# A list of single operations that runs to the 28th hidden step instead of the 16th, with six vector operations given to GpSimd

## The chip, the cores and the metric

The kernel runs on one core of one Trainium2 chip. The metric is the device time of one launch in microseconds (us), the median of several runs. A core has TensorE (PE in the profile: matrix products; PEld its weight loads), VectorE (DVE), ScalarE (ACT), GpSimd (POOL) and SyncE (SP), which here issues nearly all DMAs. Each engine works through its own instructions in the order in which they were written for it.

## What is computed

```python
def _attn_ref(x, state):                      # x: 8,8,512,64  state: 8,8,32,64
    scores = scale * x @ state^T              # softmax over the 32 states -> a
    xread = a @ state
    scores2 = scale * state @ x^T             # softmax over the 512 tokens -> a2
    sread = a2 @ x
    return concatenate([xread, sread], axis=2)
def _moe_ref(x, w_in, w_out):                 # 4352 tokens, 512 -> 2048 -> 512
    h = x @ w_in
    r = maximum(h, 0); return (r * r) @ w_out
def _moe2_ref(x, w_in, w_out, g_ln):          # 512 -> 1024 -> 512
    h = x @ w_in; solu = h * softmax(h)
    return (layernorm(solu) * g_ln) @ w_out
```

All inputs of the two feed-forward parts come in 64-bit floats; the output is 32-bit.

## The kernel before

The attention's read, `a @ state`, is never formed. For each batch the kernel multiplies `state` by the first weight matrix `w1in` (the products `sw`), and the hidden layer of a batch is then `a @ sw`. Every 32-bit operand of a matrix product is split into a high part and a low part (`high - rounded`), and a product takes three matmuls of 512 columns (lines 147 to 149 of `triple`).

**Steps.** The hidden layer of the first feed-forward part is made in steps: one step is one batch `b` and one block `f` of 128 of the 2048 hidden columns. A step has a hidden product (`hidden`, six matmuls into `ps_h`), a relu (`square`), a split of the square (`high` on ACT, `low` on DVE, tiles `gh` and `gl`), and four projections (`project`, three matmuls each into `acc`). Batches 0 and 1 take turns in chunks of four blocks, which makes the first 32 steps; batches 2 to 7 and the sread rows follow in 16 steps each.

**What the first 28 steps need besides.** 64-bit weights come by DMA as words and are turned into high and low parts (`convert_parts`, lines 215 to 232: six operations on DVE and two on ACT for each unit of 128 by 512 weights, 32 units in all, and for `w1in` a DMA that stores the result). `sw_part` multiplies state and weights, evicts on ACT (`ev_sw`, line 328) and stores to memory (`sw_d`, lines 334 to 340). `load_sw` reads a chunk back (`stg`, line 406), and `split_sw` or `split_part` splits it into `sw` (high part on ACT, low part on DVE: lines 122 and 123 when called in the list, 433 and 437 in a step). The attention of batches 0 and 1 is in `attention`, with row softmax in `rows_a` and `rows_b`; that of batch 2 is cut into parts that steps 18 to 32 hand out.

**What sets the order.** For PE, DVE, ACT and SP the order of instructions is that of the code. The first 16 steps are written as a list, `PLAN`: a piece is a letter and its indices (`H` hidden step, `G` and `L` high and low, `P` projection, `W` a state product, `V` a split of `sw`, `R`/`Q` row softmax, `i`/`o` weight conversion, `l` a load of a chunk). A piece issues one or more operations, on several engines, in one go. From step 16 the function `step` writes the order by fixed rules. GpSimd has its own order and only makes a few setup fills in the stretch spoken of here.

Of the kernel before, what the change touches and what calls it, by code (L numbers as in the profile page):

```python
# [20 lines left out]
def memory_attention_relu2_solu(  # L21
# [15 lines left out]
    nc = tc.nc  # L37
# [170 lines left out]
    def convert_parts(st, hi_r, lo_r, done=None):  # L208
# [30 lines left out]
    def convert_w1in(u, st):  # L239

        c, k = divmod(u, NM)

        t = u_tile("w1in")

        def done():
            nc.sync.dma_start(out=w1i_d[k][:, :, c * FC : (c + 1) * FC], in_=t.bitcast(F32))
            w1u[u] = t

        flying.append(convert_parts(st, t[:, 0, :], t[:, 1, :], done))

    w1o = []

    def convert_w1out(f, st):
        if f % 2 == 0:
            w1o.append(w_tile("w1out"))
        o = (f % 2) * 512
        flying.append(convert_parts(st, w1o[-1][:, 0, o : o + 512], w1o[-1][:, 1, o : o + 512]))
# [32 lines left out]
    def state_step(a, t):  # L290
# [9 lines left out]
        for i in range(2):  # L300
            if t == 0:
                split(bdw[0][:, i, :, i], bdw[0][:, i, :, 2 + i], v[:, :, :, :, i])
            else:
                o = bd[i][t]
                split(o[:, :, i], o[:, :, 1 - i], v[:, :, :, :, i])
# [4 lines left out]
    def sw_part(u, j):  # L310
# [6 lines left out]
        if at == 0:  # L317
            sw_ev[0] = evp.tile([P, 2, 512], F32, tag="ev", name="ev_sw")
        ev = sw_ev[0]
# [7 lines left out]
        triple(ps, [(lh, ll, t[:, 0, :], t[:, 1, :])], True, True)  # L327
        nc.scalar.activation(out=ev[:, at, :], in_=ps, func=AF.Copy)
        if single and j == 0:

            for b in range(2):
                if hp == 0:
                    loading[b, 0] = stgp.tile([P, 2, 512], F32, tag="stg", name="stg")
# [47 lines left out]
    def late_part(u, i):  # L381
        c, k = divmod(u, NM)
        if i == 0:
            sw_ev[0] = evp.tile([P, 2, 512], F32, tag="ev", name="ev_sw")
        ev = sw_ev[0]
# [33 lines left out]
    def split_sw(b, c):  # L419
        st = loading[b, c]  # L420
        loaded[b, c] = []
        for q in range(NQ):
            t = sw_tile("sw")
            split(t[:, 0, :], t[:, 1, :], st[:, q, :])
            loaded[b, c].append(t)
            if q == NQ - 1:
                loading.pop((b, c))
# [29 lines left out]
    def load_x(b):  # L457
        if b == 1:
            xs = wp.tile([P, NT, H, D], F32, tag="w", name="xs1")
        else:  # L460
            xs = xbuf.rearrange("p (t h d) -> p t h d", t=NT, h=H)
        for t in range(NT):
            nc.sync.dma_start(out=xs[:, t], in_=x[b].rearrange("h (p t) d -> t p h d", t=NT)[t])
        xs_t[b] = xs
# [25 lines left out]
    def attention(b):  # L490
# [5 lines left out]

        def trans_x(hp):
            if b >= 2:
                xt = atp.tile([P, S], F32, tag="st", name="xt", bufs=4)
                nc.vector.transpose(out=xt, in_=xq(hp))  # L500
                xh = xtp.tile([P, S], F32R, tag="xh", name="xh")
                xl = xtp.tile([P, S], F32R, tag="xl", name="xl")
                split(xh, xl, xt)
                v["xt", hp] = (xh, xl)
                return
            ps = ps_a.tile([P, 512], F32, tag=f"acc{hp}", name="ps_x")
            transposes(ps, [xs_t[b][:, t, 2 * hp : 2 * hp + 2].rearrange("p h d -> p (h d)") for t in range(NT)])
            if b == 0:
                xh = gp.tile([P, S], F32R, tag="gh", name="xh")
                xl = gp.tile([P, S], F32R, tag="gl", name="xl")  # L510
            else:

                if hp == 0:
                    new_a1()
                xh, xl = (a1_t[b][k][:, hp % 2, :] for k in range(2))
            v["rest", "x", hp] = split_bank(xh, xl, ps)
            v["xt", hp] = (xh, xl)

        def scores_t(hp):
            xh, xl = v.pop(("xt", hp))  # L520
# [3 lines left out]
            if b < 2:  # L524
                if i == 0:
                    v["ps", q] = bank("ps_s")
                lh, ll = (bdw[0][:, i, q, k : k + 2].rearrange("p l n b -> p (l n) b")[:, :, b] for k in (0, 2))
                triple(v["ps", q], [(lh, ll, xh, xl)], i == 0, i == 1)
                if i == 1:
                    nc.scalar.activation(out=v["st", q], in_=v["ps", q], func=AF.Copy)  # L530
                return
            ps = bank("ps_s")
            lt = bd[i][b // 2][:, q].rearrange("p l n b -> p (l n) b")[:, :, b % 2]
            nc.tensor.matmul(out=ps, lhsT=lt, rhs=xh, start=True, stop=False)
            nc.tensor.matmul(out=ps, lhsT=lt, rhs=xl, start=False, stop=True)
            n = 2 * NS
            r, o = i * n, (1 - i) * n
            st = v["st", q][r : r + n]
            nc.scalar.activation(out=st, in_=ps[o : o + n], func=AF.Copy)
            nc.vector.tensor_tensor(out=st, in0=ps[r : r + n], in1=st, op=ALU.add)  # L540
# [9 lines left out]
        def rows_a(tp):  # L550

            if b < 2:
                ps = bank("ps_r")
                by_token(tp, ps)
            else:
                ps = atp.tile([P, 512], F32, tag="e", name="e1")
                nc.vector.transpose(out=ps, in_=v["st", tp])
# [3 lines left out]
            e = atp.tile([P, 512], F32, tag="e", name="e1") if b < 2 else ps  # L561
# [3 lines left out]
            )  # L565
            nc.scalar.activation(out=e, in_=e, func=AF.Exp, scale=scale)
            v["e1", tp] = e

        def rows_b(tp):
            e3 = v["e1", tp].rearrange("p (g n) -> p g n", n=NS)  # L570
            sm = smp.tile([P, 2 * H], F32, tag="sm", name="sm")
            nc.vector.tensor_reduce(out=sm, in_=e3, axis=AX.X, op=ALU.add)
            nc.vector.tensor_scalar_add(sm, sm, 1e-9)
            nc.vector.reciprocal(out=sm, in_=sm)
            nc.vector.tensor_tensor(
# [3 lines left out]
        def cols_a(q):  # L579
# [3 lines left out]
            nc.vector.tensor_scalar_mul(mx, mx, -scale)  # L583
            sm = smp.tile([P, 1], F32, tag="cs", name="cs")
# [3 lines left out]
        def cols_b(q):  # L588
            st, sm = v["st", q], v["cs", q]
            nc.vector.tensor_scalar_add(sm, sm, 1e-9)  # L590
            nc.vector.reciprocal(out=sm, in_=sm)
            nc.scalar.activation(out=st, in_=st, func=AF.Copy, scale=sm)

        def cols_t(tp):
            ps = bank("ps_c")
            by_token(tp, ps)
            e = atp.tile([P, 2, H * NS], F32, tag="e", name="e2")
# [3 lines left out]
        def sread(half):  # L601
            if half == 0:
# [6 lines left out]
            for hp in (2 * half, 2 * half + 1):  # L609
                for t in range(NT):  # L610
                    for i in range(2):
# [7 lines left out]
                        )  # L619
            if half == 1:  # L620
                nc.scalar.activation(
# [923 lines left out]
```

## Time and profile before

| | |
|---|---|
| median of 3 runs | 1058.01 us (1054.23 to 1058.95) |
| profiled execution, its own time | 1060.5 us |
| its span, first to last instruction | 1058.7 us |
| TensorE busy | 1027.7 us, 97% of the span |
| VectorE, ScalarE, GpSimd busy | 783.9, 634.9, 138.9 us |
| hidden step 16 begins, step 28 begins | 126.5 us, 192.7 us |

The profiled execution takes 1.8 us more than its span, and 2.5 us more than the median of the runs. Matmuls are pipelined: a record of 0.39 us can begin 0.23 us after the one before, so that busy time is not the same as full use.

### The profile page before, as it was taken

How to read it: one execution, taken by the hardware profiler on the slowest of the kernel's cores; microseconds unless marked ns; L12 is line 12 of the kernel's file. 1: busy time of each engine (PE TensorE's matmuls, PEld its weight loads, DVE VectorE, ACT ScalarE, POOL GpSimd, SP SyncE). 2: the span in 40 equal slices, each digit the busy share in tenths (PEclk: the TensorE clock that was granted, in tenths of full speed). 3: DMA queues.
4: the chain of work that ended last, by engine and by line, in shares of the span. 5: the costliest groups of instructions: out<-in, count | busy, mean ns of one | idle time of the engine just before them, and what ended most of it. 6: DMA issues, size and time to landing. Idle time of an engine off the chain costs nothing.

```text
span 1058.7 us, 14931 instructions
## 1 busy us (share of the span) xinstructions
PE 1027.7 (97%) x5142; PEld 847.0 (80%) x5142; DVE 783.9 (74%) x1373; ACT 634.9 (60%) x1063; POOL 138.9 (13%) x168
## 2 busy tenths in 40 slices
PE   5899998999999999999999999999999999999998
PEld 4688776888888888888888888897888888888877
DVE  6899979777677578588686554578977877877871
ACT  6899776556556565465464443465765665666562
POOL 1000000000000000000000022222232233234110
PEclk9899999999999999999999999999999999999999
DMA  9769798387388395452531413633544444444441
GB/s 253 263 234 301 263 237 238 123 224 210 124 235 227 124 262 169 99 146 89 130 90 56 144 60 115 204 105 115 194 145 163 166 139 150 167 162 142 143 133 50
DMA packets 182956, 174.54 MB, mean 165 GB/s; under 512 B 98784, under 2 KB 132832, under 8 KB 182880
## 3 DMA queue, kind: packets, MB, share of 16 engines
q1 hardware_dynamic: 182160, 173.33, 52.9%
q8 instruction: 40, 0.66, 0.2%
q10 hardware_dynamic: 720, 0.26, 0.1%
q14 instruction: 36, 0.29, 0.1%
HBM read 106.43 MB, written 66.06 MB: 163 GB/s over the span
## 4 chain that ended last, share of the span: by engine, by line
PE 80%; DVE 9%; DMA 5%; ACT 2%; issue 2%; SPq 1%; POOL 1%; DVEq 0%; ACTq 0%; POOLq 0%
PE b L975 14%; PE acc L147 10%; PE acc L149 10%; PE acc L148 10%; PE ps_h L147 5%; PE ps_o L1118 5%; PE ps_o L1116 5%; PE ps_o L1117 5%; PE ps_h L149 5%; PE ps_h L148 5%; DMA sw_d<-ev_sw 1%; PE ps_sr L613 1%; DVE ch L225 1%; DMA st64w<-in_moe_w_in_dram 1%; DMA stg<-sw_d 1%
## 5 line engine op out<-in xcount | busy, mean ns | idle before, releaser
L147 PE MATMUL acc<-gh,w1out 128*128 128x512 f32 (+1 forms) x576 | 219.6, 381 | 2.9 <-DVE ev_x L854 1.6
L149 PE MATMUL acc<-gh,w1out 128*128 128x512 f32 (+1 forms) x576 | 217.9, 378 | 0.0
L148 PE MATMUL acc<-gl,w1out 128*128 128x512 f32 (+1 forms) x576 | 217.8, 378 | 0.0
L811 ACT ACTIVATE r<-ps_h 128x512 f32<-128x512 f32 (+1 forms) x144 | 82.1, 570 | 123.3 <-PE ps_h L149 122.5
L830 DVE TENSOR_TENSOR gl<-r,gh 128x512 fp32r<-128x512 f32 (+1 forms) x144 | 96.7, 672 | 60.1 <-ACT gh L825 53.7
L147 PEld LDWEIGHTS acc<-gh,w1out 128*128 128x128 f32 x576 | 108.7, 189 | 24.4 <-DVE ev_x L854 2.8
L149 PEld LDWEIGHTS acc<-gh,w1out 128*128 128x128 f32 x576 | 108.6, 189 | 20.5
L815 DVE TENSOR_TENSOR r<-r,ps_h 128x512 f32<-128x512 f32 (+1 forms) x120 | 77.6, 647 | 63.7 <-ACT r L811 62.8
L148 PEld LDWEIGHTS acc<-gl,w1out 128*128 128x128 f32 x576 | 108.7, 189 | 19.9
L825 ACT ACTIVATE gh<-r 128x512 fp32r<-128x512 f32 (+1 forms) x120 | 72.1, 601 | 71.2 <-DVE r L815 71.2
L1118 PE MATMUL ps_o<-w,ll 128*128 128x512 f32 x272 | 106.3, 391 | 1.3 <-DVE ll L1097 1.0
L1116 PE MATMUL ps_o<-w,lh 128*128 128x512 f32 x272 | 106.2, 390 | 0.1
L1117 PE MATMUL ps_o<-w,lh 128*128 128x512 f32 x272 | 105.9, 389 | 0.0
L149 PE MATMUL ps_h<-ah,sw 128*128 128x512 f32 x256 | 100.9, 394 | 3.4 <-DVE sw L437 2.2
L147 PE MATMUL ps_h<-ah,sw 128*128 128x512 f32 x256 | 103.0, 402 | 0.0
L148 PE MATMUL ps_h<-al,sw 128*128 128x512 f32 x256 | 100.5, 393 | 0.0
L203 POOL TENSOR_TENSOR cw<-cw,ce 128x512 f32<-128x512 f32 x16 | 20.7, 1294 | 543.9 <-DVE ce L200 500.9
L975 PE MATMUL b<-w,x2h 128*128 128x512 f32 x272 | 84.1, 390 | 0.3 <-DVE hB L993 0.3
L1048 POOL TENSOR_TENSOR var<-var,mhalf 128x1 f32<-128x1 f32 x34 | 43.6, 1281 | 234.7 <-DVE var L1047 234.5
L1118 PEld LDWEIGHTS ps_o<-w,ll 128*128 128x128 f32 x272 | 51.0, 188 | 13.4 <-DVE ll L1097 2.7
L149 PEld LDWEIGHTS ps_h<-ah,sw 128*128 128x128 f32 x256 | 48.5, 189 | 14.7 <-DVE sw L437 2.6
L1027 ACT ACTIVATE e<-hA,nm 128x1024 f32<-128x1024 f32 x17 | 19.6, 1151 | 67.2 <-DVE nm L1022 67.2
(232 smaller groups left out, 2082.9 us busy)
## 6 DMA issues: line engine op xcount, KB each, us to landing
ln_d<-ln_sq SPq DMA_DIRECT2D x32, 512.0 KB, 3.2
ln_t<-ln_d SPq DMA_DIRECT2D x128, 128.0 KB, 2.8
stg<-sw_d SPq DMA_DIRECT2D x120, 128.0 KB, 3.1
sw_d<-ev_sw SPq DMA_DIRECT2D x28, 512.0 KB, 3.5
st<-in_moe_w_out_dram SPq DMA_DIRECT2D x24, 512.0 KB, 5.2
st_x<-x_d SPq DMA_DIRECT2D x34, 256.0 KB, 3.7
w1i_d<-w1in SPq DMA_DIRECT2D x16, 512.0 KB, 4.6
st<-in_moe_w_in_dram SPq DMA_DIRECT2D x16, 512.0 KB, 5.2
```

The source lines that it names most:

```text
L147: nc.tensor.matmul(out=ps, lhsT=lh, rhs=rh, start=first and i == 0, stop=False)
L148: nc.tensor.matmul(out=ps, lhsT=lh, rhs=rl, start=False, stop=False)
L149: nc.tensor.matmul(out=ps, lhsT=ll, rhs=rh, start=False, stop=last and i == n - 1)
L811: nc.scalar.activation(out=r, in_=ps, func=AF.Relu)
L815: nc.vector.tensor_tensor(out=r, in0=r, in1=ps, op=ALU.mult)
L825: nc.scalar.activation(out=gh, in_=r, func=AF.Copy)
L830: nc.vector.tensor_tensor(out=gl, in0=r, in1=gh.bitcast(F32), op=ALU.subtract)
L975: nc.tensor.matmul(out=ps, lhsT=l, rhs=r, start=first and k == 0 and j == 0, stop=k == 1 and j == 2, skip_group_check=True,)
L1048: nc.gpsimd.tensor_tensor(out=var, in0=var, in1=mhalf, op=ALU.pow)
L1116: nc.tensor.matmul(out=ps, lhsT=a, rhs=wt[:, 0, o : o + 512], start=(k == 0), stop=False)
L1117: nc.tensor.matmul(out=ps, lhsT=a, rhs=wt[:, 1, o : o + 512], start=False, stop=False)
L1118: nc.tensor.matmul(out=ps, lhsT=bb, rhs=wt[:, 0, o : o + 512], start=False, stop=(k == NK - 1))
```

## The change

The list now goes on to the 28th step, and a piece no longer stands for a whole group of operations: each function yields after every operation or two, so that a name in the list issues the next operation of its piece, and the pieces of several engines can be interleaved one by one. The rules in `step` that served steps 16 to 27 are gone; the parts of batch 2's attention (`a...`), its loads (`q`, `h`), the partial sums read back (`x`) and the load of `gcol` (`g`) are names in the list too. Two kinds of operation change their engine: the low parts of the first state chunk (`split_sw` with `c == 0`, four operations) and the scaling of batch 0's row softmax (`rows_b` with `b == 0`, two operations) go from VectorE to GpSimd. The number of instructions on PE, ACT and SP stays the same; VectorE has six fewer and GpSimd six more.

```diff
@@ convert_parts (likewise state_step, trans_x, scores, rows_a, trans_a, hidden_part, project)
         nc.vector.tensor_scalar(out=zu, in0=hi, scalar1=0x7FFFFE00, scalar2=None, op0=ALU.bitwise_and)
+        yield 1
         nc.scalar.activation(out=zi, in_=zi, func=AF.Relu, scale=8.0, bias=rebias)
-
+        yield 1
...
@@ split_sw
-            split(t[:, 0, :], t[:, 1, :], st[:, q, :])
+            nc.scalar.activation(out=t[:, 0, :], in_=st[:, q, :], func=AF.Copy)
             loaded[b, c].append(t)
+            yield 1
+            (nc.gpsimd if c == 0 else nc.vector).tensor_tensor(
+                out=t[:, 1, :], in0=st[:, q, :], in1=t[:, 0, :].bitcast(F32), op=ALU.subtract
+            )
...
@@ rows_b
-            nc.vector.tensor_tensor(
+            yield 1
+            (nc.gpsimd if b == 0 else nc.vector).tensor_tensor(
                 out=e3, in0=e3, in1=sm.unsqueeze(2).to_broadcast([P, 2 * H, NS]), op=ALU.mult
             )
...
@@ before the list
-    nc.sync.dma_start(out=gcol, in_=g_ln.rearrange("(k p) -> p k", p=P))
...
-    when = {("o", f): w for f, w in zip(range(12, NF), (20, 21, 22, 23))}
-    when |= {("i", u): w for u, w in zip(range(3 * AHEAD + 1, NU), (16, 17, 18))}
...
@@ the list
-    I0 X0 J0 I2 i0 J2 X1 i0 U0 O0 O1 T02 T00 i0 i1 N02 T03 i2 N00 Z W00 S02 T01 N03 i2 N01 i1 i1 S00 i3 S03
...
+    I0 X0 i0 i0 i0 I2 i0 i0 i0 X0 i2 X0 i2 U0 U0 X0 i2 i2 T00 J0 i2 U0 U0 i2 i2 T01 i0 T00 T02 J2 T01 i0 i2
...
+    def piece(p):
+        if p not in steps:
+            steps[p] = parts(p[0], [int(c, 16) for c in p[1:]])
+        next(steps[p], None)
...
-    steady = range(4 * FPC, (B - 1) * NF)
+    steady = range(7 * FPC, (B - 1) * NF)
```

Three places show what this moves.

**GpSimd, from the setup fills on.** `cw`, `ce` belong to the later weight conversion. Before:

```order
masks.py:199 AFFINE_SELECT ident<-ident 128x128
L891 MEMSET a_st 128x1536
L892 MEMSET mhalf 128x1
L203 TENSOR_TENSOR cw<-cw,ce 128x512 x16
L920 TENSOR_TENSOR st_b<-st_b 128x1024 x3
```

and now:

```order
masks.py:199 AFFINE_SELECT ident<-ident 128x128
L903 MEMSET a_st 128x1536
L904 MEMSET mhalf 128x1
L587 TENSOR_TENSOR e_416<-e_416,sm 128x512
L587 TENSOR_TENSOR e_430<-e_430,sm 128x512
L435 TENSOR_TENSOR sw<-stg,sw 128x512 x4
L207 TENSOR_TENSOR cw<-cw,ce 128x512 x16
```

Six operations stand between the fills and the later conversion: the two softmax tiles of batch 0 (`e`), and then four low parts of `sw`.

**TensorE, just ahead of the first hidden product** (`ps_h`; `ps_a` are the softmax rows turned, `ps_s` scores, `ps_r` scores by token of batch 1, `ps_sw` state products). Before:

```order
L138 MATMUL ps_a_512<-ident,e_414 128x128 x2
L138 MATMUL ps_a_512<-ident,e_444 128x128 x2
L130 MATMUL ps_a_498<-ah,negi 128x512
L130 MATMUL ps_a_512<-ah,negi 128x512
L147 MATMUL ps_sw<-w1in,bd_1_189 128x512
L148 MATMUL ps_sw<-w1in,bd_1_189 128x512
L149 MATMUL ps_sw<-w1in,bd_1_189 128x512
L130 MATMUL ps_x<-ah,negi 128x512
L147 MATMUL ps_h<-ah,sw 128x512
```

and now:

```order
L147 MATMUL ps_s<-ah,bdw 128x512
L148 MATMUL ps_s<-al,bdw 128x512
L149 MATMUL ps_s<-ah,bdw 128x512
L147 MATMUL ps_s<-ah,bdw 128x512
L148 MATMUL ps_s<-al,bdw 128x512
L149 MATMUL ps_s<-ah,bdw 128x512
L516 MATMUL ps_a_532<-ah,negi 128x512
L147 MATMUL ps_sw<-w1in,bd_1_189 128x512
L148 MATMUL ps_sw<-w1in,bd_1_189 128x512
L149 MATMUL ps_sw<-w1in,bd_1_189 128x512
L558 MATMUL ps_r<-ident,st 128x128 x8
L147 MATMUL ps_h<-ah,sw 128x512
```

Batch 1's scores, its turn by token and the later state products now stand ahead of the first hidden product instead of behind it: 15 more matmuls of 512 columns (58 against 43) and eight more transposes (64 against 56).

**SyncE's queue at the fourth hidden chunk, of batches 1 and 0** (`sw_d` stores or loads of one head pair each, `stg` the chunk read back, `x2p_d` partial sums, `xs` the inputs of batch 2 or 3). Before:

```order
L406 DMA stg<-sw_d_57 64x512
L406 DMA stg<-sw_d_58 64x512
L406 DMA stg<-sw_d_59 64x512
L406 DMA stg<-sw_d_60 64x512
L170 DMA st_1865<-in_moe_w_out_dram 128x1024
L861 DMA x2p_d_117<-ev_x_1901 128x1024
L861 DMA x2p_d_117<-ev_x_1916 128x1024
L470 DMA xs<-in_x_dram 128x4x64 x4
L406 DMA stg<-sw_d_57 64x512
L406 DMA stg<-sw_d_58 64x512
L406 DMA stg<-sw_d_59 64x512
L406 DMA stg<-sw_d_60 64x512
```

and now:

```order
L353 DMA sw_d_60<-ev_sw 256x1x512
L414 DMA stg<-sw_d_57 64x512
L414 DMA stg<-sw_d_58 64x512
L414 DMA stg<-sw_d_59 64x512
L414 DMA stg<-sw_d_60 64x512
L414 DMA stg<-sw_d_57 64x512
L414 DMA stg<-sw_d_58 64x512
L414 DMA stg<-sw_d_59 64x512
L414 DMA stg<-sw_d_60 64x512
L170 DMA st_2003<-in_moe_w_out_dram 128x1024
L483 DMA xs<-in_x_dram 128x4x64 x8
L253 DMA w1i_d_65<-w1in 256x1x512
```

The second chunk's four loads stood behind a weight load, two partial sums and four input loads; they now follow the first chunk's directly. On DVE, the low part that step 24 needs was the engine's 296th instruction and is now its 285th; that of step 16 was the 228th and is the 209th, that of step 28 the 325th and the 310th.

## Rows read from the trace of the kernel before

**Rows 1.** The page: TensorE's busy time, and its granted clock in 40 slices.

```profile
PE 1027.7 (97%) x5142; PEld 847.0 (80%) x5142; DVE 783.9 (74%) x1373; ACT 634.9 (60%) x1063; POOL 138.9 (13%) x168
PEclk9899999999999999999999999999999999999999
```

**Rows 2.** Stretches: us, busy us (instructions) of each engine, granted clock, DMA share, GB/s.

```profile
0.00:8.20 8.20, 0.04 (x1) 0.07 (x2) 2.54 (x5) 2.52 (x4) 4.06 (x12) 1.00 0.82 176
8.20:30.00 21.80, 16.57 (x80) 12.03 (x80) 18.26 (x35) 17.49 (x34) 0.00 (x0) 1.00 0.99 305
30.00:40.70 10.70, 7.96 (x23) 5.57 (x24) 9.69 (x22) 7.87 (x17) 0.00 (x0) 0.58 0.68 236
40.70:120.00 79.30, 79.23 (x472) 65.00 (x472) 75.00 (x152) 70.19 (x131) 0.00 (x0) 0.99 0.76 259
120.00:180.00 60.00, 53.32 (x218) 40.99 (x217) 51.26 (x94) 41.12 (x74) 0.00 (x0) 0.97 0.87 254
```

**Rows 3.** Who PE waited for to 40.7 us: us in total, times, longest.

```profile
PE ps_st L296 <- DMA a_st<-in_state_dram: 8.2, 1, 8.2
PE ps_x L130 <- ACT ah L127: 1.8, 2, 1.0
```

**Rows 4.** PE from 123 us in order of time: start, us; in brackets idle, releaser.

```profile
128.34 0.50 PE L149 MATMUL ps_h<-ah,sw 128*128 128x512 f32 x1 [1.22 <-DVE sw L123]
155.13 0.51 PE L667 MATMUL ps_s<-xh,bd 128*128 128x512 f32 x1 [1.07 <-ACT ev_sw L328]
165.19 0.50 PE L147 MATMUL acc<-gh,w1out 128*128 128x512 f32 x1 [1.39 <-DVE ev_x L854]
174.79 0.61 PE L149 MATMUL ps_h<-ah,sw 128*128 128x512 f32 x1 [2.16 <-DVE sw L437]
```

**Rows 5.** The chain that ended last from 120 to 182 us: start, us, what.

```profile
128.92 6.60 DMA stg<-sw_d
149.58 4.82 DMA sw_d<-ev_sw
156.11 8.21 DMA sw_d<-ev_sw
170.18 3.14 DMA xs<-in_x_dram
174.04 0.70 DVE sw L437
175.83 0.43 PE ps_h L148
179.16 0.23 PE acc L148
```

**Rows 6.** The page, DMA issues: number, KB each, median us from issue to landing.

```profile
stg<-sw_d SPq DMA_DIRECT2D x120, 128.0 KB, 3.1
sw_d<-ev_sw SPq DMA_DIRECT2D x28, 512.0 KB, 3.5
```

**Rows 7.** Ahead of the first hidden step: PE and ACT in order of time.

```profile
33.17 0.69 PE L138 MATMUL ps_a<-ident,e 128*128 128x128 f32 x2 [1.26 <-DVE e L575]
39.20 0.63 PE L147 MATMUL ps_h<-ah,sw 128*128 128x512 f32 x1
38.29 0.59 ACT L131 ACTIVATE al<-ps_a 128x512 fp32r<-128x512 f32 x1
```

**Rows 8.** GpSimd's tensor operations and VectorE beside them, by time; then a group.

```profile
249.30 1.30 POOL L203 TENSOR_TENSOR cw<-cw,ce 128x512 f32<-128x512 f32 x1 [22.91 <-DVE ce L200]
249.86 1.29 DVE L697 TENSOR_TENSOR e<-e,mx 128x512 f32<-128x512 f32 x1
321.65 1.29 POOL L203 TENSOR_TENSOR cw<-cw,ce 128x512 f32<-128x512 f32 x1 [24.85 <-DVE ce L200]
322.05 0.67 DVE L740 TENSOR_REDUCE cm<-st 128x1 f32<-128x512 f32 x1
L575 DVE TENSOR_TENSOR e<-e,sm 128x512 f32<-128x512 f32 x4 | 2.8, 692 | 0.1
```

More of the change, by code (lines that the diff above doesn't have):

```diff
@@ L173, in memory_attention_relu2_solu, with run @@
     flying = []
+    def run(g):
+        for _ in g:
+            pass
     def advance():
@@ L495, in new_a1, with a1 @@
             a1_t[b] = tuple(a1p.tile([P, NQ, S], F32R, tag=t, name=t) for t in ("ah", "al"))
-        def trans_x(hp):
[L498 to L505, printed above, removed]
+        def a1():
+            if b not in a1_t:
+                new_a1()
+            return a1_t[b]
@@ L510, in trans_x, with low_x @@
+        def low_x(hp):
+            ps, xh = v["px", hp], v["xh", hp]
+            nc.tensor.matmul(out=ps, lhsT=negi, rhs=xh, start=False, stop=True, skip_group_check=True)
+            yield 1
+            if b == 0:
                 xl = gp.tile([P, S], F32R, tag="gl", name="xl")
             else:
[L513 to L517, printed above, removed]
@@ L519, in scores_t, with scores @@
-        def scores_t(hp):
-            xh, xl = v.pop(("xt", hp))
+                xl = a1()[1][:, hp % 2, :]
+            v["xl", hp] = xl
+            nc.scalar.activation(out=xl, in_=ps, func=AF.Copy)
+        def scores(hp):
+            xh, xl = v["xh", hp], v["xl", hp]
             q, i = hp // 2, hp % 2
             if i == 0:
-                v["st", q] = atp.tile([P, S], F32, tag="st", name="st", bufs=4)
[L524 to L540, printed above, removed]
@@ L601, in sread @@
         def sread(half):
-            if half == 0:
+            if "ps_sr" not in v:
                 v["ps_sr"] = bank("ps_sr")
@@ L1211, in memory_attention_relu2_solu, with hidden_part, high_part, parts @@
     done = []
-    att = [attention(0), attention(1)]
+    att, att2 = [attention(0), attention(1)], attention(2)
     steps = {}
-    hid, sq, ready, left = {}, {}, {}, {}
-    def piece(p):
-        k, a = p[0], [int(c, 16) for c in p[1:]]
+    hid, hid_ps, sq, ready, left = {}, {}, {}, {}, {}
+    def hidden_part(b, f):
+        ps = hid_ps[b, f] = hidden(b, f, loaded[b, f // FPC], *a1_t[b], S)
+        yield 1
+        r, rest = square(ps, S, f >= 3 * FPC)
+        hid[b, f] = b, f, S, r, f >= 3 * FPC
+        if f >= 3 * FPC:
+            yield 1
+            rest()
+    def high_part(b, f):
+        sq[b, f] = high(*hid[b, f])
+        r, times = hid.pop((b, f))[3:]
+        if not times:
+            yield 1
+            nc.scalar.activation(out=r, in_=r, func=AF.Square)
+    def parts(k, a):
         if k in "TNSRQABCDEF":
-            att[a[0]][k](a[1])
+            yield from att[a[0]][k](a[1])
         elif k in "io":
-            key = k, a[0]
-            if key not in steps:
-                begin(*key)
-                steps[key] = flying.pop()
-            next(steps[key], None)
+            yield from (convert_w1in if k == "i" else convert_w1out)(a[0], raw.pop((k, a[0])))
         elif k == "U":
-            state_step(a_st, a[0])
+            yield from state_step(a_st, a[0])
         elif k == "W":
-            sw_part(*a)
+            yield from sw_part(*a)
         elif k == "V":
-            key = tuple(a)
-            if key not in steps:
-                steps[key] = split_sw(*key)
-            next(steps[key], None)
+            yield from split_sw(*a)
         elif k == "H":
-            b, f = a
-            hid[b, f] = b, f, S, square(hidden(b, f, loaded[b, f // FPC], *a1_t[b], S), S, False)[0], False
-            done.append((b, f))
+            yield from hidden_part(*a)
         elif k == "G":
-            sq[a[0], a[1]] = high(*hid.pop((a[0], a[1])))
+            yield from high_part(*a)
         elif k == "L":
@@ L1502, in memory_attention_relu2_solu @@
     for m in range(4):
-        project(*pend[1], m)
+        run(project(*pend[1], m))
     sb.close()
```

246 lines of the change are left out of this document (141 added, 105 removed).

## The prediction

> **What bounds the kernel now.** I read the page first: TensorE is busy for 97% of the span, and its clock is below full in the second of 40 slices alone [rows 1]. So a change of order can only win where PE stands still or runs at the lower clock, and the next view, busy time by stretches, says where that is. PE is idle for 8.2 us to the first matmul, 5.2 of the next 21.8 us, 2.7 of the 10.7 us after that, 0.07 of 79.3 us in the middle, and 6.7 of 60 us from 120 to 180 us [rows 2]. From there to step 28 at 192.7 us, where the new list ends, it does not wait at all. In the waits of the first stretch the 8.2 us are for the state's DMA; the rest are short waits for ACT and DVE, 1.8 us in the largest group [rows 3].
>
> The four long waits after 120 us end with DVE or ACT: 1.2, 1.1, 1.4 and 2.2 us, 5.8 of the 6.7 us [rows 4]. The chain of waits shows what was late behind them. Chunk loads and stores that usually land 3.1 and 3.5 us after issue [rows 6] took 6.6, 4.8 and 8.2 us here, and the last wait ends behind a run of DVE work whose end is the low part of `sw` at 174.04 us [rows 5]. The stretch is thus limited by DVE's order and by DMAs that were asked for in a bunch, not by DVE's total: DVE is busy 51 of its 60 us [rows 2].
>
> The lower clock costs as well. At 1.2 GHz a matmul of 512 columns begins 0.43 us after the one before, at 2.4 GHz 0.23 us [rows 5]: 0.20 us for each. In the first such stretch (granted clock 0.58 from 30 to 40.7 us [rows 2]) some twelve of the 23 records are such matmuls, 2.4 us; after the 2.2 us wait at 174.79 us about eight, 1.6 us. To be had at most, then: 5.2 + 2.7 + 2.4 = 10.3 us before 40.7 us, nothing in the middle, and 6.7 + 1.6 = 8.3 us from 120 us on. The 8.2 us for the first DMA stay.
>
> **Part by part: the beginning.** No work is removed; PE, ACT and SP issue what they did. The new order puts 15 matmuls of 512 columns and eight transposes ahead of the first hidden product: 15 x 0.23 = 3.4 us, and eight of a quarter of the width, 0.5 us, together 3.9 us that PE now does in time that it waited through. Against that stands when the first hidden product can begin, 39.20 us before [rows 7]. It needs the softmax's scaled rows, which PE turns at 33.17 us right after DVE's scaling, then a split whose last piece ACT ended just before 39 us [rows 7]. In the new order ACT reaches that piece three operations later, three of 0.59 us [rows 7] or 1.8 us, but ACT was idle for 2.8 of the 10.7 us [rows 2]. The scaling runs on GpSimd: 1.29 us, as its operation on tiles of this size, against 0.69 us on DVE [rows 8], so 0.6 us more on this path. I take 0.8 us later in all (from 1.5 us earlier, if the loads that the list moves forward release it, to 3.5 us later, if nothing is absorbed: 1.8 + 0.6 and another 0.6 for the low part of `sw` with half a us of handing over). The beginning thus gives 3.9 - 0.8 = 3.1 us (0.4 to 5.4). I leave the low clock there, since PE still has many short gaps before its first hidden step; if it does not fall, 2.4 us more.
>
> **The six operations on GpSimd.** They free DVE of 6 x 0.69 = 4.1 us on paper. The trace shows what stands against this: a DVE operation with two inputs in SBUF that began beside GpSimd's took 1.29 us instead of the 0.69 us of the same form, and ended after it, while a reduction with one input beside GpSimd kept its 0.67 us [rows 8]. At 0.6 us for each of six that is 3.6 us back, so DVE gains about 0.5 us; I count nothing. The bounds are a gain of 4.1 us of DVE time, where only reductions or operations on PSUM lie beside them, and a loss of 6 x 1.29 - 4.1 = 3.6 us, where DVE stands still for all of each. The Trainium skill has this as a rule (SBUF — State Buffer, section "SBUF: two separate sides"): one pair of SBUF ports is shared by VectorE and GpSimd as an exclusive lock, which whoever comes first holds for the whole instruction. The trace agrees for two SBUF inputs; for VectorE's one-input operations in the fast mode, which the page counts in too, no row here shows it. By the page DVE would lose the 3.6 us, by the rows nothing.
>
> **From 120 us on.** Here the gain comes from order alone. Step 24 waits for a low part that was DVE's 296th instruction and is now the 285th; six of the eleven went to GpSimd, five were moved behind. At 0.69 us for a long operation and less for a short one that is some 6 us of DVE work, against a wait of 2.2 us [rows 4]. Step 16's is nineteen earlier, with a wait of 1.2 us [rows 4]. The four loads of the second chunk no longer stand behind two partial sums, which wait for an eviction, and the input loads are spread over the list, so that the bunch of DMAs behind the 8.2 us landing [rows 5] is thinner. The two waits for evictions, 1.1 and 1.4 us [rows 4], hang on that landing and are the less certain part. I take 6.5 of the 8.3 us: all but one wait of about the size of those that stand (2.5 us if only step 24's wait goes, 8.3 us if all go). What becomes late next is ACT: step 24's chunk is still loaded only some 9 us of matmuls ahead of its use, and its high parts go through ACT.
>
> **What the new order can spoil.** The middle has no idle time now. A list that names every operation binds each engine's order more tightly, and an engine that comes late by half a us holds all behind it. The old list cost 0.07 us of idle time in 79.3 us [rows 2]; I put 0.6 us against the new one (0 to 4 us, the size of the waits that stand after 120 us less the longest). `gcol`, now loaded late, is needed only at the second weights' conversion, after step 32.
>
> **Sum.** 3.1 + 0 + 6.5 - 0.6 = 9.0 us. The profiled execution of 1060.5 us would take 1051.5; its median stands 2.5 us lower, 1058.0, so the forecast is **1049.0 us**, a span of 1049.7. Its own range is 1045.5 to 1052.5.
>
> **Rivals.**
> - *More: the clock too.* The first stretch is dense enough that the clock does not fall, and nearly all waits go: 5.4 + 2.4 + 7.2 = 15 us, 1043 us. For it: the clock fell when PE had long waited in short pieces. Against: the transposes and splits of the start still alternate between PE and ACT.
> - *The beginning gives nothing.* The first hidden product comes 3.9 us later, held by ACT and GpSimd, and the rest holds: 6.5 - 0.6 = 5.9 us, less 0.4 us by which the clock stays low longer, 1052.5 us. For it: ACT has seven more operations to the first relu.
> - *Waits change places.* The chunk loads still come after stores that land late; the gaps after 120 us move to other steps, and the beginning gives 2 us: 1056 us, no change that counts. For it: DMA is 87% busy from 120 to 180 us [rows 2], and a bunch has to go somewhere.
> - *Slower: GpSimd's lock.* Up to the first hidden product five operations follow each other on GpSimd. If each first waits out a DVE operation, 5 x (1.29 + 0.69) = 9.9 us against 3.5 us on DVE puts it off by 6.4 us, 2.5 more than the 3.9 us of work moved forward; and if DVE stands still for all six, it is 3.6 us behind at 120 us, where PE already waits for it: 1058 + 6.1 = 1064 us. It decides if the first hidden product starts after about 45 us. For it: the pair at 249 us, DVE's end 0.5 us after GpSimd's [rows 8]. Against: much of DVE's work there reads PSUM or one input. [...]
>
> **Chances.** The forecast 0.48, more 0.13, nothing at the beginning 0.17, waits that change places 0.15, slower 0.07. A measurement of this kernel tells about 0.5%, 5.3 us, from no change: faster than 1052.7 us is the forecast nearly whole (0.45), the first rival and half of the second, 0.67; within it 0.26; slower 0.07. The range that holds it 8 times in 10 takes in the first rival's edge and most of the fourth's side, 1043.5 to 1056.5 us.
>
> **What would show it.** In the changed kernel's profile the first hidden product should begin near 40 us with 58 matmuls of 512 columns before it; GpSimd's six operations should take 1.3 to 2 us and some DVE operations beside them 1.2 us or more; PE's idle time from 120 us to step 28 should be under 2 us, without a low clock there, and step 28 should begin at about 183.7 us. From step 28 on the two traces should run alike. I am wrong if the first hidden product comes after 43 us, if the waits for `sw` and evictions are still there after 120 us, or if PE waits for more than 3 us between 41 and 120 us.

## The result and the profile after

The changed kernel takes 1045.43 us (median of 4 runs, 1044.1 to 1045.91) against 1057.16 us before (4 runs): a ratio of 0.989, with a 95% interval from 0.9864 to 0.9915. That is 11.7 us less. Its profiled execution takes 1045.91 us, with a span of 1044.1 us.

The page, in answer to [rows 1] (busy time; granted clock in 40 slices; the chain by engine) and [rows 6] (DMA issues):

```profile
PE 1021.6 (98%) x5142; PEld 844.4 (81%) x5142; DVE 779.0 (75%) x1367; ACT 632.6 (61%) x1063; POOL 146.3 (14%) x174
PEclk9999999999999999999999999999999999999999
...
PE 88%; DVE 5%; DMA 3%; ACT 2%; issue 1%; POOL 1%; ACTq 0%; SPq 0%; DVEq 0%; POOLq 0%
...
stg<-sw_d SPq DMA_DIRECT2D x120, 128.0 KB, 3.3
sw_d<-ev_sw SPq DMA_DIRECT2D x28, 512.0 KB, 3.4
```

The slice of lower clock is gone, and these two kinds of DMA take about as long to land as before (3.3 and 3.4 us against 3.1 and 3.5). The stretches of [rows 2] (us, busy us and instructions of PE, PEld, DVE, ACT and POOL, granted clock, DMA share, GB/s):

```profile
0.00:8.20 8.20, 0.00 (x0) 0.00 (x0) 3.05 (x7) 2.89 (x5) 4.06 (x12) 1.00 0.82 221
8.20:30.00 21.80, 18.89 (x88) 14.16 (x88) 19.36 (x42) 17.67 (x36) 1.74 (x2) 1.00 1.05 298
30.00:40.70 10.70, 9.50 (x46) 6.71 (x45) 10.47 (x16) 10.25 (x22) 4.81 (x4) 1.00 0.94 299
40.70:120.00 79.30, 76.89 (x460) 62.84 (x459) 72.11 (x148) 68.15 (x130) 1.33 (x1) 1.00 0.78 249
120.00:180.00 60.00, 60.00 (x266) 49.15 (x266) 56.56 (x111) 45.44 (x84) 0.00 (x0) 1.00 0.86 260
```

From 120 us on PE stands still for nothing: the waits of [rows 4] have no successors, and the chain there, in answer to [rows 5], is matmul after matmul. In the same 60 us PE begins 266 matmuls in place of 218, and DVE is busy 56.6 us in place of 51.3. From 30 to 40.7 us 46 records begin in place of 23, at full clock. The middle has lost, 2.4 us idle in place of 0.07. The waits that are left to 40.7 us ([rows 3]), and in the middle:

```profile
PE ps_st L303 <- DMA a_st<-in_state_dram: 9.0, 1, 9.0
PE ps_s L148 <- ACT al L540: 1.3, 1, 1.3
...
PE ps_sr L628 <- ACT e L613: 1.0, 1, 1.0
PE ps_sw L147 <- DVE e L572: 0.9, 1, 0.9
PE acc L148 <- DVE gl L843: 0.4, 1, 0.4
```

The first hidden product, in order of time, in answer to [rows 7]; it begins 0.7 us earlier than before, although 15 more matmuls and eight more transposes stand ahead of it:

```profile
37.53 1.11 PE L558 MATMUL ps_r<-ident,st 128*128 128x128 f32 x8
38.48 0.50 PE L147 MATMUL ps_h<-ah,sw 128*128 128x512 f32 x1
```

**One number for each part of the list.** In every kernel of this study 848 PE records stand ahead of step 28. From step 28 on the two kernels run alike: 1058.7 - 192.7 = 866.0 us before, 1044.1 - 178.5 = 865.6 us after. The other kernels take 865.4 to 866.9 us there, but for one with 868.0 (old list, inputs early). At the median distance from one record's start to the next (0.227 us for 512 columns, 0.109 for a transpose, 0.029 for 32 columns) the 848 take 155.3 us. What step 28 begins later than that is lost: 37.4 us before, 23.1 after. This counts short gaps and the low clock, which idle time between records does not. The table has it by stretch, worked out in the same way from each trace, good to about 0.2 us. The losses are those of the one execution that was profiled; the time in the last column is the median of all runs (us):

| kernel | first hidden | step 16 | step 28 | lost to 40 | 40 to 120 | 120 to step 28 | time |
|---|---|---|---|---|---|---|---|
| before (profiled at 1060.5) | 39.2 | 126.5 | 192.7 | 23.7 | 2.7 | 11.0 | 1057.2 |
| after | 38.5 | 119.4 | 178.5 | 18.3 | 4.5 | 0.4 | 1045.4 |
| new list, VectorE | 37.9 | 117.7 | 176.6 | 17.8 | 3.1 | 0.4 | 1046.3 |
| old list, GpSimd | 36.8 | 124.3 | 186.3 | 21.0 | 3.4 | 6.6 | 1055.2 |
| new to step 8, then old | 38.2 | 121.6 | 184.6 | 18.0 | 3.3 | 7.9 | 1054.6 |
| old to step 8, then new | 36.6 | 126.7 | 185.7 | 20.7 | 8.8 | 0.8 | 1052.3 |
| old to step 10, then new | 38.0 | 133.6 | 192.6 | 22.3 | 13.6 | 1.3 | 1059.3 |
| old list, inputs early | 37.5 | 126.2 | 190.8 | 21.6 | 4.5 | 9.3 | 1059.0 |
| old list, all loads moved | 50.3 | 160.9 | 231.5 | 27.5 | 21.1 | 27.5 | 1100.1 |
| new list, inputs late | 38.3 | 119.9 | 184.4 | 18.0 | 5.2 | 5.9 | 1052.8 |
| old list, pairs apart | 38.0 | 124.8 | 187.2 | 23.0 | 1.8 | 7.0 | 1056.1 |
| old list, step 24 split early | 38.2 | 125.1 | 188.0 | 22.8 | 2.2 | 7.7 | 1056.4 |
| new list, twelve on GpSimd | 38.0 | 117.3 | 176.2 | 17.8 | 2.9 | 0.2 | 1045.1 |
| new list, pairs adjacent | 38.4 | 120.5 | 180.7 | 18.5 | 5.4 | 1.5 | 1047.8 |

The kernel before ran between 1054.1 and 1059.8 us in the 65 runs made beside the experiments (three sets, with medians from 1056.7 to 1057.1), so its profiled execution lies above all of them.

### The profile page after: what moved, and what is told of

It is laid out like the page before. It is cut to its first block, busy times and chain, and to the rows that moved or that the text cites. A ratio compares the mean times of both kernels' runs of the same rounds, so it can differ in the third digit from the quotient of the medians.

```text
span 1044.1 us, 14955 instructions
## 1 busy us (share of the span) xinstructions
PE 1021.6 (98%) x5142; PEld 844.4 (81%) x5142; DVE 779.0 (75%) x1367; ACT 632.6 (61%) x1063; POOL 146.3 (14%) x174
## 4 chain that ended last, share of the span: by engine, by line
PE 88%; DVE 5%; DMA 3%; ACT 2%; issue 1%; POOL 1%; ACTq 0%; SPq 0%; DVEq 0%; POOLq 0%
PE b L986 14%; PE acc L147 11%; PE acc L148 11%; PE acc L149 11%; PE ps_h L147 6%; PE ps_h L149 6%; PE ps_h L148 6%; PE ps_o L1129 5%; PE ps_o L1128 5%; PE ps_o L1127 5%; PE ps_sr L628 2%; DMA w1i_d<-w1in 1%; DMA st_x<-x_d 1%; PE ps_sw L399 1%; PE ps_sw L400 1%
## 5 line engine op out<-in xcount | busy, mean ns | idle before, releaser
L838 ACT ACTIVATE gh<-r 128x512 fp32r<-128x512 f32 (+1 forms) x144 | 87.2, 606 | 71.2 <-DVE r L832 70.0
L148 PEld LDWEIGHTS acc<-gl,w1out 128*128 128x128 f32 x576 | 108.4, 188 | 20.7 <-DVE gl L843 0.8
L207 POOL TENSOR_TENSOR cw<-cw,ce 128x512 f32<-128x512 f32 x16 | 20.7, 1296 | 483.1 <-DVE ce L204 417.3
L1127 PEld LDWEIGHTS ps_o<-w,lh 128*128 128x128 f32 x272 | 51.1, 188 | 11.0 <-ACT lh L1102 0.6
```

The source lines that it names most:

```text
L148: nc.tensor.matmul(out=ps, lhsT=lh, rhs=rl, start=False, stop=False)
L838: nc.scalar.activation(out=gh, in_=r, func=AF.Copy if times else AF.Square)
L1127: nc.tensor.matmul(out=ps, lhsT=a, rhs=wt[:, 0, o : o + 512], start=(k == 0), stop=False)
```

## The experiments

For the lists, the old order was written in the new names, each old piece as its single operations in a row and steps 16 to 27 as the old rules issue them; on every engine that is the instruction order of the kernel before. A mixed list takes one list up to a name and then what is left in the other's order.

**The order alone.** New list, six operations on VectorE:

```diff
-            (nc.gpsimd if c == 0 else nc.vector).tensor_tensor(
+            nc.vector.tensor_tensor(
...
-            (nc.gpsimd if b == 0 else nc.vector).tensor_tensor(
+            nc.vector.tensor_tensor(
```

> The new list with all six operations back on VectorE, so the order alone. My theory (order gives the gain, the move to GpSimd is worth nothing net): 1045.4 us as with the full change, within 2 us, and step 28 again near 178.5 us. Rival 'lock' (GpSimd's operations hold VectorE up by what they relieve it of, and more): 3 to 4 us faster, 1042 us. Rival 'relief' (VectorE's load is what had to go): at least 4 us slower, 1049.5 us or more, with waits for VectorE back after 120 us.

Measured: 1046.29 us, ratio 0.9897 (0.9879 to 0.9915). The order is the change; the six operations are worth less than the runs can tell.

```profile
30.00:40.70 10.70, 10.18 (x43) 7.62 (x42) 9.57 (x19) 10.04 (x21) 0.00 (x0) 0.84 1.02 351
40.70:120.00 79.30, 77.93 (x465) 63.99 (x465) 73.54 (x152) 69.53 (x133) 0.00 (x0) 1.00 0.79 253
120.00:180.00 60.00, 60.00 (x267) 49.29 (x266) 56.26 (x110) 45.35 (x83) 0.00 (x0) 1.00 0.83 257
```

These are its windows. PE does not wait after 120 us with the six on VectorE either, so they were not what step 24 waited behind.

**GpSimd alone.** The old order with the six on GpSimd:

```diff
-    I0 X0 i0 i0 i0 I2 i0 i0 i0 X0 i2 X0 i2 U0 U0 X0 i2 i2 T00 J0
+    g0 I0 X0 X0 X0 X0 J0 I2 i0 i0 i0 i0 J2 X1 X1 X1 X1 i0 i0 U0
...
```

> The old order of every other engine's instructions, with the six operations on GpSimd: the other half of the change by itself. My theory: no difference from the kernel before, 1057 us within 3 us; the 2.2 us wait at step 24 shrinks at most by a part, since the six operations lie 100 us ahead of it. Rival 'lock': 3 to 6 us slower, 1060 to 1063 us, the first hidden product after 41 us. Rival 'relief': 3 to 4 us faster, 1053 us.

Measured: 1055.16 us, ratio 0.9991 (0.9979 to 1.0002): no difference that the runs can tell. Its waits from 120 us on:

```profile
PE ps_h L149 <- DVE sw L435: 2.8, 2, 2.2
PE acc L147 <- DVE ev_x L868: 0.7, 1, 0.7
PE ps_s L685 <- DVE xl L676: 0.5, 1, 0.5
```

The 2.2 us wait for `sw` at step 24 stands as before. Neither "lock" (3 to 6 us slower) nor "relief" (3 to 4 us faster) holds; the interval leaves room for 2 us less.

**The two parts of the list.** New to step 8, then old:

```diff
 ... q23 P111 P110 L12
-    H14 i8 F01 ib D10 C11 ib P122 H15 o4 D11 Ka
+    i4 P033 i9 U3 U3 ib ib ib V01 V01 W90 W90 P122 i8 i8 i8 H14 H14 Ka
```

> The new order up to the first matmul of the ninth hidden step (step 8), and behind it all remaining operations in the old order; the six operations stay on GpSimd. My theory (two gains that do not depend on each other): the beginning's gain alone, 5 to 6 us by the matmul spacing of the trace after, so 1051.5 us; first hidden product near 38.5 us, no low clock in the beginning, and idle time of 4 to 7 us again between 120 us and step 28. Rival 'one gain' (the late waits go because everything runs ahead, whatever the order there): 1046 to 1047 us, idle time after 120 us under 2 us.

and the reverse, old to step 8, then new:

```diff
 ... V01 W90 W90 P122 G13 G13 i8 i8 i8 i8
-    H14 H14 E01 E01 Ka L13 P120 G14 G14
+    C10 E01 E01 F00 C10 F01 C11 q23 H14 F01 D10 C11 H15 o4
```

> The old order up to the first matmul of step 8, and behind it all remaining operations in the new order; the six operations on GpSimd. My theory: the late gain alone, 6.5 to 9 us, so 1049.5 us within 2 us, with the low clock still there in the beginning and no wait over 1 us after 120 us. Rival 'one gain': 1055 us or more, waits for sw and for evictions still there after 120 us.

Measured: 1054.57 us (0.9979, 0.9966 to 0.9992) and 1052.32 us (0.9959, 0.9943 to 0.9975). By the table each half has its own stretch: with the old order behind step 8, 7.9 us are lost after 120 us even behind the new beginning; with the new order 0.8 us even behind the old one. "One gain" falls. But the medians give 2.3 and 4.5 us, 6.8 of 11.7, each some 3 us less than was expected, so the two gains do not simply add up. Behind the new beginning the old order loses 7.9 us after 120 us, against 6.6 behind its own with the same six operations on GpSimd. In the reverse list the rest went at the seam, where PE in the timeline waited for a softmax copy and then ran 6.8 us at the lower clock (512 columns every 0.43 us):

```profile
83.00 3.06 PE L628 MATMUL ps_sr<-e,xs 128*64 128x32 f32 x56 [1.85 <-ACT e L613]
...
86.58 0.63 PE L148 MATMUL ps_h<-al,sw 128*128 128x512 f32 x1
87.01 0.63 PE L149 MATMUL ps_h<-ah,sw 128*128 128x512 f32 x1
```

**A seam without that clump**, at step 10, where the lists have done nearly the same (the old order up to `H16`, then the new):

```diff
 ... W80 P141 O8 W81 W81 W81 P143 L15
-    H16 H16 P151 O9 ia ia ia o6 o6 o6 o6 E11 E11 L17
+    q23 q20 H04 H16 o6 a020 o6 ia ia H16 Wb1 o7 Wb1 o7
```

> As the run that kept the old order to step 8, but with the seam at step 10, where the two lists have done nearly the same operations, so that no clump of transposed reads stands at the seam. If what that run lost against the full change was the seam's own stall and the low clock after it (5.9 us by the spacing of matmuls): 1047 to 1049 us, no stall over 1 us at 85 to 100 us. If the late order only works behind the new beginning: 1052 us as before, and waits after 100 us.

Measured: 1059.34 us (1.0026, 1.0016 to 1.0036). The expectation failed, but not for its rival's reason: behind 120 us only 1.3 us are lost. At this seam VectorE came to turn batch 2's inputs, as the new list has it, before the loads, which the old list issues late, had landed:

```profile
96.77 0.42 DVE L219 TENSOR_SCALAR cz<-st 128x512 uint32<-128x512 uint32 x1
105.49 0.71 DVE L668 STREAM_TRANSPOSE xt<-xs 128x512 f32<-128x512 f32 x1 [8.30 <-DMA xs<-in_x_dram]
```

VectorE stood for 8.3 us, and PE then waited 4.1 and 3.8 us for `gl` and `w1in`, which stand behind it. In this list and in the one before, PE lost much before 120 us (13.6 and 8.8 us by the table), and the other engines and the DMAs could get ahead in that time. That so little is lost after 120 us is therefore not shown to be the work of the late order alone. The wait for the inputs asked for the next three runs.

**Batch 2's inputs.** The old order (VectorE) with the four input loads (`q`) alone as early as the new list or the buffer allows, in the places where they went in and came out:

```diff
 V01 V01 F01 F01
+q20 q23
 G15 G15 O6 O7
...
 Ke Kf l12 x00
-q20 q21
 G07 G07 H08 L07
```

then the old order with every load that stands alone in the list (`I` to `O`, `X`, `Z`, `g`, `l`, `q`, `x`, `h`) at the new list's place, from the first on; then the new list with the inputs late, as at the second (its turn is `a120`; three of the four loads move back, one comes a step earlier):

```diff
 o6 H05 Kc o7
-q21
 P150 o6 Wa1 W81
...
 U2 P040 P050 H07
+q21
 a120 o8 V02 o9
```

> The old order and VectorE for the six operations; the only edit is that the four loads of batch 2's inputs are issued where the new list has them, or as soon as batch 0's last read of that buffer is over (step 10 to 15 in place of 16 to 18). Theory 'inputs' (in the old order VectorE stands in its queue for the late inputs, and the low part of sw for step 24 stands behind it): the 2.2 us wait at step 24 and the low clock after it go, 1053 us within 1.5. Rival 'VectorE's order' (the low part is simply too far back): 1056 to 1057 us, the wait still over 1.5 us, and VectorE busy ahead of it.

> The old order on TensorE, VectorE and ScalarE, and every load that stands alone in the list issued at the new list's place. If the order of the loads carries the late gain: 1049 to 1051 us. If it is the order of the operations on VectorE and ScalarE: no more than the inputs alone give, 1053 us or above.

> The full change, but batch 2's inputs are loaded late: each just ahead of the VectorE operation that turns it, or where the old list has it (step 13, 16 and 18 in place of 11, 14 and 8; the third a step earlier). Theory 'inputs': VectorE waits 2 to 4 us for each of three loads, TensorE loses 3 to 6 us of it, 1049 to 1051 us. Rival: VectorE has that much slack in the new order, 1045 to 1046.5 us.

Measured: 1058.95 us (1.0021, 1.0011 to 1.0031), 1100.09 us (1.0414, 1.0397 to 1.043) and 1052.83 us (0.9965, 0.9954 to 0.9977). PE's waits in the first, from 120 us on, and in the second, from 20 us on:

```profile
PE ps_h L149 <- DVE sw L435: 3.6, 2, 2.1
PE ps_sw L147 <- ACT ev_sw L340: 1.9, 1, 1.9
```

```profile
PE ps_h L147 <- ACT sw L432: 11.1, 1, 11.1
PE ps_x L138 <- DMA xs<-in_x_dram: 9.2, 2, 5.2
PE acc L148 <- DVE gl L843: 5.3, 1, 5.3
```

VectorE, and PE at step 16, in the third, in order of time:

```profile
120.66 0.71 DVE L668 STREAM_TRANSPOSE xt<-xs 128x512 f32<-128x512 f32 x1 [4.64 <-DMA xs<-in_x_dram]
...
123.66 0.50 PE L149 MATMUL ps_h<-ah,sw 128*128 128x512 f32 x1 [2.44 <-DVE sw L435]
...
131.56 0.72 DVE L668 STREAM_TRANSPOSE xt<-xs 128x512 f32<-128x512 f32 x1 [2.75 <-DMA xs<-in_x_dram]
```

So the early inputs are a condition of the new order: without them it gives back 7.4 us, VectorE stands 4.6 and 2.8 us for two of them, and the wait for `sw` is back, 2.4 us at step 16. In the old order they do nothing for step 24. There VectorE did not stand for them: in the kernel before it waits 0.4 us for `xs` in all from 120 us to step 28. The time fits neither expectation: it is 2.3 us longer than before, clear of noise. Its trace takes 2 us more than the others behind step 28, and why stays open. All the new places of the loads in the old order of the operations cost 43 us: in these runs the loads fit only the order that they were written with.

**VectorE's order and VectorE's time**, each by one edit in the old order:

```diff
+        nc.vector.tensor_scalar(out=uu, in0=hi, scalar1=0x1FF, scalar2=None, op0=ALU.bitwise_and)
         nc.vector.tensor_scalar(out=zu, in0=hi, scalar1=0x7FFFFE00, scalar2=None, op0=ALU.bitwise_and)
         nc.scalar.activation(out=zi, in_=zi, func=AF.Relu, scale=8.0, bias=rebias)
-        nc.vector.tensor_scalar(out=uu, in0=hi, scalar1=0x1FF, scalar2=None, op0=ALU.bitwise_and)
         nc.vector.scalar_tensor_tensor(out=u, in0=lo, scalar=2.0**-32, in1=uu, op0=ALU.mult, op1=ALU.add)
```

> The kernel before with one edit: in the weight conversion the second mask is made ahead of the first, so that the VectorE operation that reads the second mask no longer stands directly behind the one that makes it. In the traces that operation took 0.69 us directly behind its producer (kernel before) and 0.62 us with another operation between (kernel after). 32 units by 0.07 us is 2.2 us less VectorE work up to step 28. Theory 'VectorE's time' (it sets TensorE's pace from 120 us on): 1054.5 to 1055.5 us. Rival 'order and loads alone': 1056 to 1057 us, no difference that can be measured.

```diff
-  V13 oe oe oe oe P180 oe oe P181 oe oe P182 P183 G1a G1a a500 H1b a510 a520 L1a a521 a522 V13 H1b V13 V13
+  V13 V13 oe oe oe oe P180 oe oe P181 oe oe P182 P183 V13 V13 G1a G1a a500 H1b a510 a520 L1a a521 a522 H1b
```

> The old order, six operations on VectorE; the only edit is that the chunk of step 24 is split earlier: the first low part directly behind its high part in step 22, the second pair at the end of step 22 in place of step 23. That takes some seven VectorE operations out from in front of it. Theory 'VectorE's order': the 2.2 us wait at step 24 and the 1.6 us of low clock behind it go, 1053 to 1054 us. Rival 'the wait moves' (VectorE is as far behind as before and the next operation that needs it waits): 1056 to 1057 us, with a wait of about 2 us at another place before step 28.

Measured: 1056.07 us (0.9997, 0.9985 to 1.0009) and 1056.35 us (0.9997, 0.9985 to 1.0008): neither differs from the kernel before. VectorE's operations up to step 28 take 164.4 us with the pairs apart against 167.1 before (each counted from the end of the one before it), and nothing comes of it. With the early split the 2.2 us wait is indeed gone, and others stand in its place. PE's waits from 120 us to step 28:

```profile
PE ps_h L149 <- DVE sw L435: 1.4, 1, 1.4
PE acc L148 <- DVE gl L843: 1.2, 2, 0.9
PE acc L147 <- DVE ev_x L868: 0.9, 2, 0.7
PE ps_s L685 <- DVE xl L676: 0.5, 1, 0.5
PE acc L147 <- ACT gh L838: 0.5, 1, 0.5
```

The `sw` left is step 16's; at steps 24 and 25 PE now waits 0.3, 0.5 and 0.9 us for `gl` and `gh`. "The wait moves" holds.

**Two tests on the new list.** Twelve operations on GpSimd, and the pairs adjacent again:

```diff
-            (nc.gpsimd if c == 0 else nc.vector).tensor_tensor(
+            (nc.gpsimd if c <= 1 else nc.vector).tensor_tensor(
...
-            (nc.gpsimd if b == 0 else nc.vector).tensor_tensor(
+            nc.gpsimd.tensor_tensor(
```

> The full change with the suspected cost doubled: the second state chunk's four low parts and batch 1's two softmax scalings go to GpSimd too, twelve operations in all. By the sums of VectorE's operations in the traces the first six relieve it of 3.9 us and stretch other operations by 4.9 us. If that is right, twelve cost a little: 1045 to 1047.5 us. Rival 'lock': each new operation holds TensorE's supply up, 1049 us or more. Rival 'relief': 1043 us or less.

```diff
 O1 i3 W20 S00
-i1
 N02 X1
+i1
 i1 i3 i3 S01
...
```

> The full change, but in every weight conversion the two operations that feed one VectorE operation directly are put next to it again in the list, as the old list had them (second mask and its use, exponent and its use). Two pairs in each of 32 units, 0.07 us each, add up to 4 us of VectorE work before step 28, where VectorE has some 9 us of idle time from step 8 on. Theory 'VectorE's time': 1047 to 1049 us. Rival: hidden, 1045 to 1046 us.

Measured: 1045.13 us (0.9894, 0.9875 to 0.9912), no difference from six; and 1047.79 us (0.9923, 0.9906 to 0.9941), 2.4 us more than the full change, its six runs (1047.22 to 1051.05) all above the latter's four. Only VectorE's order differs between these two kernels: 35 of its operations move. They now take 163.5 us up to step 28, against 160.2 in the full change (and 161.8 with twelve on GpSimd, where it cost nothing). The moved operations also stand at other places in VectorE's queue, so that this run does not tell VectorE's time from its order. The window from 120 us on, with VectorE idle for 3.1 of 60 us against 3.4 in the full change:

```profile
120.00:180.00 60.00, 59.89 (x260) 47.94 (x259) 56.94 (x108) 45.05 (x82) 0.00 (x0) 1.00 0.85 261
```

## Why the prediction was right, and where it was off

**The beginning**, 3.9 - 0.8 = 3.1 us, and 2.4 us more if the clock does not fall. The first hidden product came at 38.5 us, against 39.2 before and 37.5 to 38.2 in three other traces of the old order without GpSimd (inputs early, pairs apart, early split): 0.3 to 1.0 us later than theirs, where 0.8 was forecast. The clock did not fall after all (1.00 from 30 to 40.7 us), so the term that was left out belongs in: 3.1 + 2.4 = 5.5 us, and 23.7 - 18.3 = 5.4 us were measured to 40 us. That the two agree so well is in part luck. Leaving out the run with all loads moved, the lists with the old beginning lose 20.7 to 23.7 us to 40 us and those with the new one 17.8 to 18.5, so the gain is 2.2 to 5.9 us by the pair that one takes. The granted clock from 30 to 40.7 us was 0.52 to 0.84 in the former and 0.84 to 1.00 in the latter, and the new list with VectorE lost no more at 0.84 (17.8) than the full change at 1.00. One term was too small: the eight transposes, put at 0.5 us, take 0.9 at 0.109 us each.

**The six operations**, nothing net. Right, by both runs that test it (new list on VectorE, old list with GpSimd), and twelve cost nothing either. GpSimd's operations and VectorE's beside them, in order of time, in answer to [rows 8]:

```profile
26.28 1.05 POOL L587 TENSOR_TENSOR e<-e,sm 128x512 f32<-128x512 f32 x1 [21.65 <-DVE sm L585]
26.32 0.68 DVE L582 TENSOR_REDUCE sm<-e 128x16 f32<-128x512 f32 x1
29.31 1.05 POOL L587 TENSOR_TENSOR e<-e,sm 128x512 f32<-128x512 f32 x1 [1.99 <-DVE sm L585]
29.36 1.28 DVE L237 TENSOR_SCALAR cz<-ch 128x512 uint32<-128x512 uint32 x1
30.32 3.13 POOL L435 TENSOR_TENSOR sw<-stg,sw 128x512 fp32r<-128x512 f32 x2
30.68 1.64 DVE L239 SCALAR_TENSOR_TENSOR w1out<-cu,cz 128x512 fp32r<-128x512 f32 x1
32.36 1.38 DVE L219 TENSOR_SCALAR cz<-st64w 128x512 uint32<-128x512 uint32 x1
37.04 1.36 POOL L435 TENSOR_TENSOR sw<-stg,sw 128x512 fp32r<-128x512 f32 x1 [3.59 <-ACT sw L432]
37.29 1.39 DVE L237 TENSOR_SCALAR cz<-ch 128x512 uint32<-128x512 uint32 x1
39.38 0.42 DVE L237 TENSOR_SCALAR cz<-ch 128x512 uint32<-128x512 uint32 x1
...
50.03 1.33 POOL L435 TENSOR_TENSOR sw<-stg,sw 128x512 fp32r<-128x512 f32 x1 [11.63 <-ACT sw L432]
50.12 1.78 DVE L843 TENSOR_TENSOR gl<-r,gh 128x512 fp32r<-128x512 f32 x1
```

Beside GpSimd the one-input mask takes 1.28 to 1.39 us in place of the 0.42 us that it takes alone at 39.38, and the two-input operation 1.64 in place of 0.69; the reduction at 26.32 keeps its 0.68. These four stretches add up to 0.86 + 0.95 + 0.96 + 0.97 = 3.7 us, and the `gl` at 50.12, 1.78 us in place of the 0.68 it takes elsewhere, adds 1.1: 4.8 us against the 4.1 us taken off. The Trainium skill's rule (SBUF — State Buffer, "SBUF: two separate sides": the pair of ports shared by VectorE and GpSimd is held by one of them for a whole instruction) agrees with this trace for the one-input masks too, which the prediction had left open. The net loss that the prediction worked out under it, 3.6 us, was too much. One of the six began beside a reduction, and VectorE went on with it; each of the other five cost VectorE 0.9 to 1.1 us, less than its own 1.05 to 1.71 us. The prediction's 0.6 us for each was too little (4.8 / 6 = 0.8), but 0.7 us more of VectorE's time here does not show in the time of the kernel.

**From 120 us on**, 6.5 of 8.3 us. The mechanism holds (order alone; all waits gone), the size does not for these two traces. The cap was read from idle time between records and a count of slow matmuls; by starts of matmuls the stretch lost 11.0 us, and 10.6 of it came back. In two other traces of the old order (pairs apart, early split) it lost 7.0 and 7.7 us, of which 6.6 and 7.3 would have come back. So the term was too small for the execution that it was read from, and near to what a more typical one had to give, which is luck. "All but one wait" was too careful. One reason given fails: that six of the eleven instructions that left the front of step 24's low part did so by going to GpSimd. With the six back on VectorE the wait is gone just the same, and with the six on GpSimd in the old order it stands. Nor was the distance of that part the point: moved forward in the old order, it only hands its wait on. What carries the gain is the new order of operations with its loads as a whole; the inputs' early loads are a shown condition of it, that VectorE's queue still limits it is shown too (pairs adjacent), though not whether by its time or its order; which other moves matter stays open.

**The middle**, -0.6 us (0 to -4): 4.5 us are lost against 2.7, so -1.8. Over all traces with one list throughout (without all loads moved), the old order loses 1.8 to 4.5 us here and the new 2.9 to 5.4, so the size is uncertain. Of the signs named ahead, the others came too: waits of 2.4 us in all from 41 to 120 us, none behind, GpSimd's six at 1.05 to 1.7 us (two below the 1.3 forecast), the same course from step 28 on; that step came at 178.5 us, 5.2 us ahead of the forecast.

**Sum.** 5.4 + 10.6 - 1.8 = 14.2 us between the two profiled executions, where 9.0 was forecast; their spans differ by 14.6. The medians differ by 11.7, because the execution that was read lay at the upper edge: the two old-order runs of which a trace near the median exists (pairs apart, early split) lose 31.8 and 32.7 us, 8.7 and 9.6 more than the changed kernel. By the terms as these two traces have them, the forecast's 9.0 us is close, with terms that erred against each other: 4.5 to 4.7 us at the beginning, 6.6 to 7.3 late, 2.3 to 2.7 lost in the middle. The time of 1045.43 us lies just outside the forecast's own range (from 1045.5) and nearer to "more: the clock too" (1043 us) than to 1049; the gain of 11.7 us is nearer to 9.0 than to that rival's 15, since the kernel before now had a median of 1057.16 us, not 1058.01. That rival's cause is half right: the clock stayed up and every late wait went, but the middle gave some back. "Slower" and "the beginning gives nothing" are ruled out by the first hidden product at 38.5 us, "waits change places" by the empty list of waits after 120 us; as a mechanism it is what met the single edits of the old order.

## What to carry to other kernels

Measure a stretch by the starts of its matmuls against their own spacing, not by idle time, and ask whether the execution that was profiled is a typical one. Moving forward the one instruction that is waited for can only pass the wait on, as it did here at step 24; the new order paid as a whole, together with the loads that it needs, and parts of it cost more than none (the seam at step 10, the loads alone). Moving work from VectorE to GpSimd bought nothing here, where VectorE had one- and two-input SBUF operations to run beside it.

## What the runs showed of the hardware

- In these rows a VectorE operation that reads what the one just before it wrote begins only after that one's end; one that does not begins before it. VectorE in the run with the early split, the first mask, the second and its use, in order of time; then the same three operations in the run with the pairs apart, where the second mask is made first:

```profile
156.84 0.43 DVE L219 TENSOR_SCALAR cz<-st 128x512 uint32<-128x512 uint32 x1
157.18 0.42 DVE L225 TENSOR_SCALAR cu<-st 128x512 uint32<-128x512 uint32 x1
157.64 0.69 DVE L227 SCALAR_TENSOR_TENSOR cu<-st,cu 128x512 f32<-128x512 uint32 x1
```

```profile
155.92 0.43 DVE L217 TENSOR_SCALAR cu<-st 128x512 uint32<-128x512 uint32 x1
156.27 0.42 DVE L218 TENSOR_SCALAR cz<-st 128x512 uint32<-128x512 uint32 x1
156.60 0.68 DVE L221 SCALAR_TENSOR_TENSOR cu<-st,cu 128x512 f32<-128x512 uint32 x1
```

The use begins 0.46 us after the start of the operation just before it where it reads what that wrote, and 0.33 us where it does not: 0.13 us for this pair. Over all operations up to step 28 VectorE's time is 2.7 us shorter with the pairs apart.
- How far the runs of one kernel spread differs: 3.7 to 5.6 us in sets of 12 to 23 runs of the old late order (before, old list with GpSimd, inputs early, new to step 8, pairs apart, early split), 1.7 to 2.0 us in 4 or 5 runs of the new one (the full change, VectorE, twelve on GpSimd). The waits after 120 us are not shown to be the reason: the new list with late inputs loses 5.9 us there and spreads over 1.6 us in 6 runs, and pairs adjacent loses 1.5 us and spreads over 3.8.
- GpSimd's product of 128 by 512 values with a scale per group took 1.05 us, its difference of two full tiles 1.33 to 1.71 us, all beside VectorE.
